# Another seven-product scheme: four products through one PSUM bank that is read in between

## The chip, the core and the metric

The kernel runs on one core of a Trainium2 chip. Its engines work in parallel, each through its own queue in order: TensorE (PE, matmuls into PSUM banks), VectorE (DVE), ScalarE (ACT), GpSimd (POOL, here issuing loads) and SyncE (SP, here issuing stores). The metric is device time in microseconds (us) of one execution; lower is better.

## The reference

```python
scores = scale * np.matmul(q, k.transpose(0, 1, 3, 2))     # q, k, v: (8, 12, 448, 64)
attn = softmax(scores)
x = np.matmul(attn, v).transpose(0, 2, 1, 3).reshape(3584, 768)
h = x @ w_in                                               # (768, 2048)
g = h * (1.0 / (1.0 + np.exp(-h)))
out = g @ w_out                                            # (2048, 768), float32
```

Attention for 8 batches of 12 heads and 448 tokens, then a two-layer network over all 3584 tokens.

## The kernel before, in words

Operands are fp16, sums fp32 in PSUM. Attention for a batch is made in units of four heads: scores (line 336), exponentials on ACT (373), sums and values on PE (399, 415), and a normalisation on DVE (482) into `xT`. For batches 0 to 5 the first layer is plain: six matmuls of 128 x 448 for each of 16 slices f of the hidden layer (496), a tanh on ACT (507), a gate on DVE (543), into the gate buffer `G` (`X` for a few tokens).

**Seven products.** Elsewhere a product of two-by-two blocks is computed with seven block products instead of eight. The blocks are combined by sums beforehand and the seven results are combined afterwards. This is done in two places:

- *the pair stage* (first layer of the last two batches, `PB` = 6 and 7): the blocks are the two batches and the two halves of the 768 inputs against two halves of inputs and hidden slices. For each f from 0 to 7 there are seven products of three matmuls of 128 x 448 (`pair_product`, line 632), copies on ACT (`pair_copy`, 657), sums on DVE (`pair_add`, 663), and four gates on ACT (`silu`, 670). The weight and input sums are `combine_w_in` (608) and `combine_x` (590).
- *the quads* (second layer, 13 of 14 groups of 2 x 128 tokens, `qd` 1 to 13; group 0 is plain, 718): seven products of eight matmuls of 128 x 384 (`product`, 704) with summed weights (`combine_w`, 533) and summed gate outputs (`combine_g`, 694). Three ACT copies (770, 776, 780) and six DVE additions (766) make the four output blocks, which are stored by 32 or 64 tokens (`store`, 762).

A PSUM bank holds one such result. In the pair stage banks A and C are separate one-bank tiles (tag "m", four of them), and B and D are the two halves of a two-bank tile (tag "s", two of them, which hold the scores before). `PBANK` and `BANK` say which product goes into which bank; a product that is not first in its bank adds to what is there.

**What sets the order.** A planner written in Python (`Order`) runs when the program is built. It keeps a clock of its own, assumed durations for every operation, and counts of free buffers and banks (`Ring`). Whenever PE is free it issues the first item of the list `moe` whose dependencies are done and whose buffers are free, or attention work; ACT and DVE take the ready operation with the earliest due time (ready time plus a bias). The engines then get exactly this order. On the chip the semaphores are set by the tile framework from the tiles that the operations read and write, not from the planner's dependencies. Stores are issued by SP, for the last two quads by ACT in turn with SP.

Of the kernel before, what the change touches and what calls it, by code (L numbers as in the profile page):

```python
# [165 lines left out]
def kernel(  # L166
# [42 lines left out]
    NSG, NTMP, NOST = 3, 3, 4  # L209
# [307 lines left out]
    W_ = {m: const.tile([128, HF, OH], FP16, name=f"D{m}") for m in (1, 4, 6)}  # L517
# [4 lines left out]
    }  # L522
    W_[3], W_[7], W_[5], W_[2] = B_[0, 1], B_[1, 0], B_[1, 1], B_[0, 0]

    def combine_w(m, f0, f1):
        i0, i1, op = {
            1: ((0, 0), (1, 1), ALU.add),
            4: ((1, 0), (0, 0), ALU.subtract),
            6: ((0, 0), (0, 1), ALU.add),
            3: ((0, 1), (1, 1), ALU.subtract),  # L530
            7: ((1, 0), (1, 1), ALU.add),
        }[m]
        nc.vector.tensor_tensor(
            out=W_[m][:, f0:f1], in0=B_[i0][:, f0:f1], in1=B_[i1][:, f0:f1], op=op
        )
# [75 lines left out]
    PBANK = {1: "A", 2: "A", 6: "B", 5: "C", 3: "C", 7: "D", 4: "D"}  # L611

    def pair_product(f, m):
        if m in (1, 5):
            pp_t[(f, PBANK[m])] = ps.tile(
                [128, 512], FP32, name=f"f_{f}_{m}", tag="m", bufs=4
            )[:, 0:S]
        elif m == 6:
            two = ps.tile([128, 2, 512], FP32, name=f"f_{f}_{m}", tag="s", bufs=2)
            pp_t[(f, "B")], pp_t[(f, "D")] = two[:, 0, 0:S], two[:, 1, 0:S]  # L620
# [10 lines left out]
        for c in range(3):  # L631
            nc.tensor.matmul(  # L632
                out=pp_t[(f, PBANK[m])],
                lhsT=w[:, c, :],
                rhs=a[:, c, :],
                start=(c == 0 and m in (1, 6, 5, 7)),
                stop=(c == 2),
                skip_group_check=True,
            )

    def pair_tmp(f, name):
# [4 lines left out]
            "v": ("T", NT_, [128, HG, S], FP16),  # L646
        }[name]
        t = sb.tile(shape, dt, name=f"{name}_{f}", tag=tag, bufs=n)
        if len(shape) == 5:
            t = t.rearrange("p c x i e -> p (c x i e)")  # L650
        elif len(shape) == 3:
            t = t.rearrange("p h s -> p (h s)")
# [6 lines left out]
    def pair_add(f, to, x, y):  # L659
        x = pp_t[(f, x)] if x in "BCD" else pf_t[(f, x)]  # L660
        y = pf_t[(f, y)]
        out = pf_t[(f, to)] if (f, to) in pf_t else pair_tmp(f, to)
        nc.vector.tensor_tensor(out=out, in0=x, in1=y, op=ALU.add)
# [13 lines left out]
    S_t, tmp_t, ost_t, pr_t = {}, {}, {}, {}  # L677

    def combine_g(qd, m, f0, f1):
        a, b = 2 * qd, 2 * qd + 1  # L680
        x, y, op = {
            5: (rows(a, 0), rows(a, 1), ALU.add),
            2: (rows(b, 0), rows(b, 1), ALU.add),
            1: (rows(a, 0), rows(b, 1), ALU.add),
            6: (rows(b, 0), rows(a, 0), ALU.subtract),
            7: (rows(a, 1), rows(b, 1), ALU.subtract),
        }[m]
        if m > 5:
            dst = x
        else:  # L690
            if (qd, m) not in S_t:
                S_t[(qd, m)] = sb.tile([128, HF, 128], FP16, name=f"S_{qd}_{m}", tag="S", bufs=NSG)
            dst = S_t[(qd, m)]
        nc.vector.tensor_tensor(out=dst[:, f0:f1], in0=x[:, f0:f1], in1=y[:, f0:f1], op=op)  # L694

    BANK = {3: 3, 5: 3, 4: 4, 2: 4, 1: 1, 7: 1, 6: 6}

    def product(qd, m):
        w = {3: rows(2 * qd, 0), 4: rows(2 * qd + 1, 1), 6: rows(2 * qd + 1, 0), 7: rows(2 * qd, 1)}
# [34 lines left out]
    def tmp(qd, name):  # L734
        tmp_t[(qd, name)] = sb.tile([128, OH], FP32, name=f"{name}_{qd}", tag="tmp", bufs=NTMP)
        return tmp_t[(qd, name)]

# [27 lines left out]
    def add(out, a, b, op=ALU.add):  # L765
        nc.vector.tensor_tensor(out=out, in0=a, in1=b, op=op)  # L766


    def take_3(qd):
        nc.scalar.copy(out=tmp(qd, "s"), in_=bank(qd, 3))  # L770

    def take_4(qd):
        add(tmp_t[(qd, "s")], bank(qd, 4), tmp_t[(qd, "s")])

    def take_5(qd):
        nc.scalar.copy(out=ost(qd, 0, 1), in_=bank(qd, 3))  # L776
        store(qd, 0, 1)

    def take_2(qd):
        nc.scalar.copy(out=ost(qd, 1, 0), in_=bank(qd, 4))  # L780
        store(qd, 1, 0)

    def take_1(qd):
        add(tmp(qd, "m"), bank(qd, 1), tmp_t[(qd, "s")])

    def less_12(qd):
        add(tmp_t[(qd, "s")], tmp_t[(qd, "s")], ost_t[(qd, 0, 1)], ALU.subtract)

    def less_21(qd):
        add(tmp_t[(qd, "m")], tmp_t[(qd, "m")], ost_t[(qd, 1, 0)], ALU.subtract)  # L790

    def take_6(qd):
        add(ost(qd, 1, 1), bank(qd, 6), tmp_t[(qd, "m")])
        store(qd, 1, 1)

    def take_7(qd):
        add(ost(qd, 0, 0), bank(qd, 1), tmp_t[(qd, "s")])
        store(qd, 0, 0)
# [113 lines left out]
    sg_ring, tmp_ring, ost_ring = Ring(NSG), Ring(NTMP), Ring(NOST)  # L912
    far_ring = Ring(NX3)
    STORE = 3.0
    pr_op, sg_op, w_op, plain_op = {}, {}, {2: [], 5: []}, {}
# [3 lines left out]
    def queue_ffn1(b, g0, g1):  # L919
        t0, t1 = 32 * g0, 32 * g1  # L920
        for f in range(NFF) if b == 0 else [x for f in range(HF) for x in (f, f + HF)]:
# [22 lines left out]
            def deps(f=f):  # L944
# [3 lines left out]
                for qd in range(NT * B // 4) if u else ():  # L948
                    if any(t // NT == u - 1 and (r or t % NT < 4) for t in (2 * qd, 2 * qd + 1)):
# [3 lines left out]
                            else [pr_op.get((qd, m)) for m in (3, 4, 6, 7)]  # L953
# [56 lines left out]
    def queue_pair_f(f, xs):  # L1010
        done, lo = {}, f // 4 * 4

        def free(r):
            made = []
            for qd in range(NT * B // 4):
                for t in (2 * qd, 2 * qd + 1):
                    if t // NT == PB // 2 - 1 and t % NT < (4, NT - 1)[r]:
                        made += [pr_op.get((qd, m)) for m in (3, 4, 6, 7)]
# [10 lines left out]
        def queue(m):  # L1029
            rings = {  # L1030
                1: ((rq_ring, 1),),
                6: ((s_ring, 1), (kt_ring, 1), (t_ring, 1)),
                5: ((rk_ring, 1),),
            }.get(m, ())
            ms = (6, 7) if m == 6 else (m,)

            def run():
                op = Op(
                    "PE",
                    3 * len(ms) * mm(S),  # L1040
                    lambda: [pair_product(f, x) for x in ms],
                    tail=PE_OUT,
                )
                if m in (1, 5):
                    m_ring.take()
# [6 lines left out]
                elif m == 6:  # L1052
                    read("u", "DVE", lambda: pair_add(f, "u", "B", "p"), [op, done["p"]])
                    read("v", "DVE", lambda: pair_add(f, "v", "D", "u"), [op, done["u"]])
                elif m == 5:
                    read("q", "ACT", lambda: pair_copy(f, "q", "C"), [op], None, -3)
                    read("22", "DVE", lambda: pair_add(f, "v", "q", "v"), [done["v"], done["q"]], rk_ring.give)
                    gate_of(1, 1, "v", [done["22"]], t_ring.give)
                elif m == 2:
                    gate_of(0, 0, "A", [op], m_ring.give)  # L1060
                elif m == 3:
                    read("12", "DVE", lambda: pair_add(f, "p", "C", "u"), [op, done["u"]], m_ring.give)
                    gate_of(1, 0, "p", [done["12"]], rq_ring.give)
                else:
                    read("21", "DVE", lambda: pair_add(f, "u", "D", "u"), [op, done["12"]], s_ring.give)
                    gate_of(0, 1, "u", [done["21"]], kt_ring.give)

            def deps():
                made = [xs[0, c] for c in (range(3, NDC) if m == 2 else range(3))]
                if m in (5, 6):  # L1070
                    made += [pair_x[i] for i in ((2, 3) if m == 6 else (1,))]
                    made += [pair_w.get((i, lo)) for i in ((2, 3) if m == 6 else (1,))]
                elif m == 3:
                    made.append(pair_x[4])
                elif m == 4:
                    made.append(pair_w.get((4, lo)))
                made += [done.get(x) for x in {2: ["p"], 3: ["q"], 4: ["v"]}.get(m, [])]
                first = {3: (2, 5), 4: (3,), 5: (6,), 6: (1,)}.get(m, ())
                made += [(done.get(x), 9.0) for x in first]
                return made + (free(0) if m == 1 else free(1) if m == 6 else [])  # L1080

            moe.append((deps, int(m in (1, 5)), run, rings))

        for m in (1, 6, 5, 2, 3, 4):
            queue(m)

    def sums_w(ms):

        for m in ms:
# [6 lines left out]
                        ld_wout + list(plain_op.values()) * (m in (3, 7)),  # L1096
# [6 lines left out]
    def queue_plain(t, j):  # L1103
# [6 lines left out]
        def queue(f0, f1):  # L1110
            def run():
# [10 lines left out]
                if len(plain_op) == 4:  # L1122
                    sums_w((3, 7))
# [22 lines left out]
    def plan_sums():  # L1146
# [12 lines left out]
        for m in (5, 2, 1, 6, 7):  # L1159
            sg_op[(qd, m)] = []  # L1160
            for f0 in (0, 4):
                deps = [x for f in range(f0, f0 + 4) for x in gates[f] + gates[f + HF]]
                if m > 5:
                    deps += sg_op[(qd, {6: 2, 7: 5}[m])]
# [12 lines left out]
    def queue_quad(qd):  # L1177
# [4 lines left out]
        def read(m, eng, fn, deps, then=None):  # L1182
            if m in (5, 2):
                then = lambda at: (m_ring.give(at), home.give(at + STORE))
            elif m in (6, 7):
                then = lambda at: (m_ring.give(at), home.give(at + STORE), tmp_ring.give(at))
            busy = act(OH) if eng == "ACT" else OH / 960.0 + 0.13
            bias = -2 if eng == "ACT" else -4
            took[m] = od.add(Op(eng, busy, lambda: fn(qd), deps, bias, then=then))

        def queue(m, first):
            def run():
# [5 lines left out]
                if m in (5, 2, 1):  # L1198
# [3 lines left out]
                if m == 3:  # L1202
                    read(3, "ACT", take_3, [op])
                elif m == 4:
                    read(4, "DVE", take_4, [op, took[3]])
                elif m == 5:
                    read(5, "ACT", take_5, [op], m_ring.give)
                elif m == 2:
# [375 lines left out]
```

## Time and profile before

| | us |
|---|---|
| three runs | 395.9, 396.16, 396.45; median 396.16 |
| profiled execution, span from first to last instruction | 394.4 (its time beyond the span is not given) |
| PE busy | 386.5 (98%) |
| DVE, ACT busy | 311.3 (79%), 243.2 (62%) |
| quad products, L704 / pair products, L632, share of the chain that ended last | 29% / 8% |
| copy of 384 columns on ACT (L776, L780, L770) | 0.48 each |
| copy of 448 columns on ACT (L657) | 0.53 each |
| addition of 384 columns on DVE (L766) | 0.55 each |
| addition of 448 columns on DVE (L663) | 0.62 each |

A row of the profile names the line of the kernel, the engine, the operation, the tile written and the tiles read, then the count and the time. Idle time in front of a row stands in brackets with what ended it. The chain that ended last is the sequence of work that is followed back from the last instruction. A busy PE is not necessarily PE at its peak, since matmuls overlap: a matmul's own duration is longer than the distance to the next one.

### The profile page before, as it was taken

The numbers are of one execution on the slowest core, as the hardware profiler recorded it, in microseconds if no ns is written. First come the engines' busy times: TensorE is split into PE (matmuls) and PEld (weight loads), VectorE is DVE, ScalarE is ACT, GpSimd is POOL, SyncE is SP. The second block draws the span as 40 slices with busy tenths as digits, with TensorE's granted clock in tenths as the row PEclk, the third lists the DMA queues.
The fourth block names the chain that finished last, engine by engine and source line by source line (L and its number), as shares of the span: only waits on it lengthen the run. The fifth ranks groups of instructions, "written<-read, shape, count | busy, mean of one in ns | idle before, by whom it ended". The sixth has DMA issues, their size and how long they took to land.

```text
span 394.4 us, 9273 instructions
## 1 busy us (share of the span) xinstructions
PE 386.5 (98%) x3679; PEld 199.0 (50%) x3679; DVE 311.3 (79%) x653; ACT 243.2 (62%) x378; POOL 83.6 (21%) x153
## 2 busy tenths in 40 slices
PE   7999999999999999999999999999999999999995
PEld 6667764443444444554444444344444555556663
DVE  2466676999999697896888786988879898787863
ACT  4988885696863868626868429686593227872110
POOL 6632546315004242500051221120000000000000
PEclk9999999999999999999999999999999999999999
DMA  7999999919034863582145751531100131001334
GB/s 113 205 210 210 166 179 164 175 36 141 1 76 88 142 95 47 75 158 71 25 49 81 139 109 46 71 48 42 42 1 2 40 87 35 2 1 42 80 82 121
DMA packets 35356, 34.44 MB, mean 87 GB/s; under 512 B 11376, under 2 KB 33776, under 8 KB 35312
## 3 DMA queue, kind: packets, MB, share of 16 engines
q0 software_dynamic: 24784, 22.82, 39.2%
q1 hardware_dynamic: 9952, 10.33, 9.6%
q10 hardware_dynamic: 576, 0.69, 0.6%
q8 instruction: 29, 0.48, 0.5%
q14 instruction: 15, 0.12, 0.1%
HBM read 45.61 MB, written 11.01 MB: 144 GB/s over the span
## 4 chain that ended last, share of the span: by engine, by line
PE 94%; DMA 3%; DVE 1%; ACT 1%; POOL 0%; issue 0%; POOLq 0%
PE p L704 29%; PE h L496 29%; PE s L336 12%; PE a L399 10%; PE f L632 8%; PE o L718 3%; DMA rq<-in_q_dram 3%; PE a L415 2%; PE z L1491 1%; ACT E L373 0%; DVE S L694 0%; POOL rk L249 0%; DVE rq L323 0%; DVE rdn L466 0%; DVE ost L766 0%
## 5 line engine op out<-in xcount | busy, mean ns | idle before, releaser
L373 ACT ACTIVATE E<-s 128x896 f16<-128x896 f32 (+1 forms) x172 | 150.0, 915 | 48.6 <-PE s L336 47.5
L496 PE MATMUL h<-xT,w_in_t 128*128 128x448 f16 (+1 forms) x672 | 118.6, 327 | 0.0
L496 PEld LDWEIGHTS <-w_in_t 128*128 128x128 f16 x672 | 61.2, 98 | 54.0 <-issue 18.0
L507 ACT ACTIVATE th<-h 128x448 f16<-128x448 f32 (+1 forms) x112 | 54.3, 495 | 31.4 <-PE h L496 22.5
L543 DVE SCALAR_TENSOR_TENSOR G<-th,h 128x448 f16<-128x448 f16 (+2 forms) x112 | 55.1, 507 | 15.3 <-ACT th L507 13.3
L270 POOL DMA_DIRECT2D V<-in_v_dram x88 | 48.5, 568 | 56.5 <-PE a L399 42.7
L336 PE MATMUL s<-rq,KT 32*128 32x448 f16 (+4 forms) x768 | 50.9, 337 | 1.4 <-DVE rq L323 0.9
L704 PEld LDWEIGHTS <-G 128*128 128x128 f16 x384 | 36.5, 98 | 28.1 <-issue 4.4
L704 PEld LDWEIGHTS <-S 128*128 128x128 f16 x312 | 29.3, 98 | 23.9 <-issue 5.2
L399 PE MATMUL a<-E,V 128*32 128x448 f16 (+3 forms) x864 | 40.4, 335 | 0.0
L255 POOL DMA_DIRECT2D rq<-in_q_dram x27 | 15.1, 560 | 113.0 <-PE s L336 82.9
L704 PE MATMUL p<-D,G 128*128 128x384 f16 x208 | 37.6, 326 | 0.0
L704 PE MATMUL p<-w_out_t,S 128*128 128x384 f16 x208 | 37.2, 326 | 0.1
L482 DVE SCALAR_TENSOR_TENSOR xT<-a,rdn 128x448 f16<-128x448 f32 (+1 forms) x54 | 28.7, 565 | 7.4 <-PE a L399 6.5
L336 PEld LDWEIGHTS <-KT 32*128 32x128 f16 (+2 forms) x864 | 17.5, 98 | 29.6 <-issue 25.9
L704 PE MATMUL p<-w_out_t,G 128*128 128x384 f16 x176 | 31.9, 326 | 0.0
L399 PEld LDWEIGHTS <-V 128*32 128x32 f16 (+2 forms) x864 | 18.2, 95 | 22.4 <-issue 14.7
L384 DVE TENSOR_TENSOR T<-T,E 128x1792 f16<-128x1792 f16 x20 | 21.8, 1089 | 8.0 <-ACT E L373 7.9
L694 DVE TENSOR_TENSOR S<-G 128x512 f16<-128x512 f16 x70 | 25.3, 414 | 3.2 <-PE p L704 3.0
L384 DVE TENSOR_TENSOR T<-E,E 128x1792 f16<-128x1792 f16 x20 | 21.6, 1082 | 5.6 <-ACT E L373 5.6
L776 ACT COPY ost<-p 128x384 f32<-128x384 f32 x13 | 6.2, 480 | 27.4 <-PE p L704 22.6
L305 DVE STREAM_TRANSPOSE KT<-rk 128x256 f32<-128x256 f32 (+3 forms) x48 | 16.6, 384 | 7.0 <-DMA rk<-in_k_dram 6.2
(74 smaller groups left out, 370.2 us busy)
## 6 DMA issues: line engine op xcount, KB each, us to landing
out_dram<-ost SPq DMA_DIRECT2D x194, 48.0 KB, 1.7
rk<-in_k_dram POOLq DMA_DIRECT2D x24, 224.0 KB, 5.9
rq<-in_q_dram POOLq DMA_DIRECT2D x21, 224.0 KB, 5.2
w_in_t<-in_moe_w_in_dram POOLq DMA_DIRECT2D x6, 512.0 KB, 11.2
w_out_t<-in_moe_w_out_dram POOLq DMA_DIRECT2D x4, 768.0 KB, 13.5
V<-in_v_dram POOLq DMA_DIRECT2D x43, 64.0 KB, 3.9
V<-in_v_dram POOLq DMA_DIRECT2D x40, 48.0 KB, 4.0
out_dram<-ost SPq DMA_DIRECT2D x8, 96.0 KB, 2.2
```

The source lines that it names most:

```text
L270: nc.gpsimd.dma_start(out=VT[b][32 * x : 32 * (x + 1), hs, 0:count, :], in_=v[b, hs].rearrange("h (i g) d -> i h g d", g=TPP)[:, :, first ...
L336: nc.tensor.matmul(out=pS[p0 : p0 + 32 * (x1 - x0), h % 2, at : at + nq], lhsT=KT[(b, hg)][32 * h : 32 * (h + 1), c, x0:x1, :, e], rhs=QT[ ...
L373: nc.scalar.activation(out=E[(n, w)][0:kr, 2 * y : 2 * y + 2, 0:nk], in_=pS_t[(n, w, y)][0:kr, :, 0:nk], func=AF.Exp, scale=attn_scale,)
L384: nc.vector.tensor_tensor(out=T[n], in0=T[n] if step else E[(n, 0)], in1=E[(n, step + 1)], op=ALU.add,)
L399: nc.tensor.matmul(out=a[32 * h : 32 * (h + 1), 0:nq], lhsT=w, rhs=e[k0:k1, h, at : at + nq], start=start, stop=stop,)
L482: nc.vector.scalar_tensor_tensor(out=x3(b, cc)[:, cc % 3, 32 * g0 : 32 * g1], in0=acc[(n, part)][:, 0:nq], scalar=0.5, in1=rdn_t[n].rearra ...
L496: nc.tensor.matmul(out=h[:, 0 : t1 - t0], lhsT=w_in_t[:, cc, 128 * f : 128 * (f + 1)], rhs=x3(b, cc)[:, cc % 3, t0:t1], start=(cc == 0), s ...
L507: nc.scalar.activation(out=th, in_=h_t[(b, f, t0)][:, 0 : t1 - t0], func=AF.Tanh)
L543: nc.vector.scalar_tensor_tensor(out=dst[:, f, at + lo : at + hi], in0=th_t[(b, f, t0)][:, lo - t0 : hi - t0], scalar=1.0, in1=h_t[(b, f, ...
L632: nc.tensor.matmul(out=pp_t[(f, PBANK[m])], lhsT=w[:, c, :], rhs=a[:, c, :], start=(c == 0 and m in (1, 6, 5, 7)), stop=(c == 2), skip_gro ...
L694: nc.vector.tensor_tensor(out=dst[:, f0:f1], in0=x[:, f0:f1], in1=y[:, f0:f1], op=op)
L704: nc.tensor.matmul(out=pr_t[(qd, BANK[m])][:, 0:OH], lhsT=w[:, f, :], rhs=W_[m][:, f, :], start=(f == 0 and BANK[m] == m), stop=(f == HF - 1),
```

## The change

The seven products are formed after another scheme, in both places. Its sums build on one another: a second sum is made from the first one and a third from the second. In the quads four sums of gate outputs take the place of five and four sums of weights the place of five. Products 1, 6, 7 and 4 follow one another in one bank. Its content is read after 1, after 6 (1 + 6), after 7 (1 + 6 + 7) and after 4 (all four). Product 2 has a bank of its own, and 5 and 3 share one. Three DVE additions per quad (for 2, 7, 3) and four ACT copies (for 1, 5, 6, 4) take the place of six and three.

In the pair stage the same scheme is used: three copies (p after 1, u after 6, q after 5) and three additions (p += B after 2, q += A after 7, u += C after 3) take the place of two and five. Banks A (1, 6, 7, 4) and B (2) are the halves of the two-bank tile, and C (5, 3) is a one-bank tile; bank D is gone.

The planner's queueing follows: one item per product, in the order 1, 5, 6, 2, 7, 3, 4. The output buffers `ost` grow from four to seven and the three `tmp` buffers go.

```diff
-    NSG, NTMP, NOST = 3, 3, 4
+    NSG, NOST = 3, 7
...
-    W_[3], W_[7], W_[5], W_[2] = B_[0, 1], B_[1, 0], B_[1, 1], B_[0, 0]
+    W_[1], W_[2], W_[3], W_[7] = B_[0, 0], B_[1, 0], B_[1, 1], B_[0, 1]
...
+            5: (B_[0, 1], B_[0, 0]),
+            6: (B_[1, 1], W_[5]),
+            4: (B_[1, 0], W_[6]),
+            7: (B_[1, 1], B_[0, 1]),
...
-    PBANK = {1: "A", 2: "A", 6: "B", 5: "C", 3: "C", 7: "D", 4: "D"}
+    PBANK = {1: "A", 6: "A", 7: "A", 4: "A", 2: "B", 5: "C", 3: "C"}
...
-        if m in (1, 5):
-            pp_t[(f, PBANK[m])] = ps.tile(
-                [128, 512], FP32, name=f"f_{f}_{m}", tag="m", bufs=4
-            )[:, 0:S]
-        elif m == 6:
+        if m == 5:
+            pp_t[(f, "C")] = ps.tile([128, 512], FP32, name=f"f_{f}_{m}", tag="m", bufs=4)[:, 0:S]
+        elif m == 1:
             two = ps.tile([128, 2, 512], FP32, name=f"f_{f}_{m}", tag="s", bufs=2)
-            pp_t[(f, "B")], pp_t[(f, "D")] = two[:, 0, 0:S], two[:, 1, 0:S]
+            pp_t[(f, "A")], pp_t[(f, "B")] = two[:, 0, 0:S], two[:, 1, 0:S]
...
-    def pair_add(f, to, x, y):
-        x = pp_t[(f, x)] if x in "BCD" else pf_t[(f, x)]
-        y = pf_t[(f, y)]
-        out = pf_t[(f, to)] if (f, to) in pf_t else pair_tmp(f, to)
-        nc.vector.tensor_tensor(out=out, in0=x, in1=y, op=ALU.add)
+    def pair_add(f, to, x):
+        t = pf_t[(f, to)]
+        nc.vector.tensor_tensor(out=t, in0=pp_t[(f, x)], in1=t, op=ALU.add)
...
+            5: (rows(b, 0), rows(b, 1), ALU.add),
+            6: (S_t.get((qd, 5)), rows(a, 0), ALU.subtract),
+            7: (rows(a, 0), rows(b, 0), ALU.subtract),
+            3: (rows(a, 1), S_t.get((qd, 6)), ALU.subtract),
...
-    BANK = {3: 3, 5: 3, 4: 4, 2: 4, 1: 1, 7: 1, 6: 6}
+    BANK = {1: 1, 6: 1, 7: 1, 4: 1, 2: 2, 5: 5, 3: 5}
...
+    OUT = {1: (0, 0), 5: (1, 1), 6: (0, 1), 4: (1, 0)}
+    SUM = {2: (0, 0), 7: (1, 1), 3: (0, 1)}
+
+    def take_copy(qd, m):
+        nc.scalar.copy(out=ost(qd, *OUT[m]), in_=bank(qd, BANK[m]))
+        if m == 4:
+            store(qd, *OUT[m])
+
+    def take_sum(qd, m):
+        t = ost_t[(qd, *SUM[m])]
+        nc.vector.tensor_tensor(out=t, in0=bank(qd, BANK[m]), in1=t, op=ALU.add)
+        store(qd, *SUM[m])
...
             rings = {
-                1: ((rq_ring, 1),),
-                6: ((s_ring, 1), (kt_ring, 1), (t_ring, 1)),
+                1: ((s_ring, 1), (rq_ring, 1)),
                 5: ((rk_ring, 1),),
+                6: ((kt_ring, 1),),
             }.get(m, ())
...
+                elif m == 6:
+                    read("u", "ACT", lambda: pair_copy(f, "u", "A"), [op], None, -3)
                 elif m == 2:
-                    gate_of(0, 0, "A", [op], m_ring.give)
+                    read("11", "DVE", lambda: pair_add(f, "p", "B"), [op, done["p"]])
+                    gate_of(0, 0, "p", [done["11"]], rq_ring.give)
+                elif m == 7:
+                    read("22", "DVE", lambda: pair_add(f, "q", "A"), [op, done["q"]])
+                    gate_of(1, 1, "q", [done["22"]], rk_ring.give)
                 elif m == 3:
-                    read("12", "DVE", lambda: pair_add(f, "p", "C", "u"), [op, done["u"]], m_ring.give)
-                    gate_of(1, 0, "p", [done["12"]], rq_ring.give)
+                    read("12", "DVE", lambda: pair_add(f, "u", "C"), [op, done["u"]], m_ring.give)
+                    gate_of(1, 0, "u", [done["12"]], kt_ring.give)
                 else:
-                    read("21", "DVE", lambda: pair_add(f, "u", "D", "u"), [op, done["12"]], s_ring.give)
-                    gate_of(0, 1, "u", [done["21"]], kt_ring.give)
+                    gate_of(0, 1, "A", [op, done["11"]], s_ring.give)
...
+                made += [
+                    done.get(x)
+                    for x in {6: ["p"], 7: ["u", "q"], 3: ["q"], 4: ["22", "11"]}.get(m, [])
+                ]
...
-        for m in (1, 6, 5, 2, 3, 4):
+        for m in (1, 5, 6, 2, 7, 3, 4):
             queue(m)
```

More of the change, by code (lines that the diff above doesn't have):

```diff
@@ L516 @@
     X = const.tile([128, NFF, 128], FP16, name="X")
-    W_ = {m: const.tile([128, HF, OH], FP16, name=f"D{m}") for m in (1, 4, 6)}
+    W_ = {m: const.tile([128, HF, OH], FP16, name=f"D{m}") for m in (4, 5, 6)}
     B_ = {
@@ L522 @@
     }
-    W_[3], W_[7], W_[5], W_[2] = B_[0, 1], B_[1, 0], B_[1, 1], B_[0, 0]
+    W_[1], W_[2], W_[3], W_[7] = B_[0, 0], B_[1, 0], B_[1, 1], B_[0, 1]
     def combine_w(m, f0, f1):
[L526 to L531, printed above, removed]
+        x, y = {
+            5: (B_[0, 1], B_[0, 0]),
+            6: (B_[1, 1], W_[5]),
+            4: (B_[1, 0], W_[6]),
+            7: (B_[1, 1], B_[0, 1]),
         }[m]
         nc.vector.tensor_tensor(
-            out=W_[m][:, f0:f1], in0=B_[i0][:, f0:f1], in1=B_[i1][:, f0:f1], op=op
+            out=W_[m][:, f0:f1], in0=x[:, f0:f1], in1=y[:, f0:f1], op=ALU.subtract
         )
@@ L635, in pair_product @@
                 rhs=a[:, c, :],
-                start=(c == 0 and m in (1, 6, 5, 7)),
+                start=(c == 0 and m in (1, 2, 5)),
                 stop=(c == 2),
@@ L645, in pair_tmp @@
             "u": ("KT", 3, [128, NCH, 4, 32, 2], FP16),
-            "v": ("T", NT_, [128, HG, S], FP16),
         }[name]
@@ L650, in pair_tmp @@
             t = t.rearrange("p c x i e -> p (c x i e)")
-        elif len(shape) == 3:
-            t = t.rearrange("p h s -> p (h s)")
         pf_t[(f, name)] = t[:, 0 : 2 * S].bitcast(FP32)
@@ L675, in silu @@
         )
-    S_t, tmp_t, ost_t, pr_t = {}, {}, {}, {}
+    S_t, ost_t, pr_t = {}, {}, {}
     def combine_g(qd, m, f0, f1):
         a, b = 2 * qd, 2 * qd + 1
+        if m != 7 and (qd, m) not in S_t:
+            S_t[(qd, m)] = sb.tile([128, HF, 128], FP16, name=f"S_{qd}_{m}", tag="S", bufs=NSG)
         x, y, op = {
[L682 to L686, printed above, removed]
-        }[m]
[L688 to L693, printed above, removed]
+            5: (rows(b, 0), rows(b, 1), ALU.add),
+            6: (S_t.get((qd, 5)), rows(a, 0), ALU.subtract),
+            7: (rows(a, 0), rows(b, 0), ALU.subtract),
+            3: (rows(a, 1), S_t.get((qd, 6)), ALU.subtract),
+        }[m]
+        dst = rows(b, 0) if m == 7 else S_t[(qd, m)]
         nc.vector.tensor_tensor(out=dst[:, f0:f1], in0=x[:, f0:f1], in1=y[:, f0:f1], op=op)
-    BANK = {3: 3, 5: 3, 4: 4, 2: 4, 1: 1, 7: 1, 6: 6}
+    BANK = {1: 1, 6: 1, 7: 1, 4: 1, 2: 2, 5: 5, 3: 5}
     def product(qd, m):
-        w = {3: rows(2 * qd, 0), 4: rows(2 * qd + 1, 1), 6: rows(2 * qd + 1, 0), 7: rows(2 * qd, 1)}
+        w = {1: rows(2 * qd, 0), 2: rows(2 * qd, 1), 4: rows(2 * qd + 1, 1), 7: rows(2 * qd + 1, 0)}
         w = w[m] if m in w else S_t[(qd, m)]
@@ L732, in bank @@
         return pr_t[(qd, m)][:, 0:OH]
-    def tmp(qd, name):
-        tmp_t[(qd, name)] = sb.tile([128, OH], FP32, name=f"{name}_{qd}", tag="tmp", bufs=NTMP)
-        return tmp_t[(qd, name)]
     def ost(qd, i, j):
@@ L763, in store @@
             w, turn = w + n, turn + 1
[L765 to L798, printed above, removed]
+    OUT = {1: (0, 0), 5: (1, 1), 6: (0, 1), 4: (1, 0)}
[8 more added lines that the diff above has]
+        store(qd, *SUM[m])
     units = []
@@ L911 @@
     ffn1_left = {b: 0 for b in range(B)}
-    sg_ring, tmp_ring, ost_ring = Ring(NSG), Ring(NTMP), Ring(NOST)
+    sg_ring, ost_ring = Ring(NSG), Ring(NOST)
     far_ring = Ring(NX3)
     STORE = 3.0
-    pr_op, sg_op, w_op, plain_op = {}, {}, {2: [], 5: []}, {}
+    pr_op, sg_op, w_op, plain_op = {}, {}, {1: [], 2: [], 3: []}, {}
     inv_op, norm_op = [], []
@@ L952, in deps @@
                             if qd == 0
-                            else [pr_op.get((qd, m)) for m in (3, 4, 6, 7)]
+                            else [pr_op.get((qd, m)) for m in (1, 2, 3, 4, 7)]
                         )
@@ L1017, in free @@
                     if t // NT == PB // 2 - 1 and t % NT < (4, NT - 1)[r]:
-                        made += [pr_op.get((qd, m)) for m in (3, 4, 6, 7)]
+                        made += [pr_op.get((qd, m)) for m in (1, 2, 3, 4, 7)]
             return made
@@ L1030, in queue @@
             rings = {
-                1: ((rq_ring, 1),),
-                6: ((s_ring, 1), (kt_ring, 1), (t_ring, 1)),
+                1: ((s_ring, 1), (rq_ring, 1)),
                 5: ((rk_ring, 1),),
+                6: ((kt_ring, 1),),
             }.get(m, ())
-            ms = (6, 7) if m == 6 else (m,)
             def run():
[L1038 to L1044, printed above, removed]
+                op = Op("PE", 3 * mm(S), lambda: pair_product(f, m), tail=PE_OUT)
+                if m == 5:
                     m_ring.take()
@@ L1051, in run @@
                     read("p", "ACT", lambda: pair_copy(f, "p", "A"), [op], None, -3)
-                elif m == 6:
-                    read("u", "DVE", lambda: pair_add(f, "u", "B", "p"), [op, done["p"]])
-                    read("v", "DVE", lambda: pair_add(f, "v", "D", "u"), [op, done["u"]])
                 elif m == 5:
                     read("q", "ACT", lambda: pair_copy(f, "q", "C"), [op], None, -3)
-                    read("22", "DVE", lambda: pair_add(f, "v", "q", "v"), [done["v"], done["q"]], rk_ring.give)
-                    gate_of(1, 1, "v", [done["22"]], t_ring.give)
+                elif m == 6:
+                    read("u", "ACT", lambda: pair_copy(f, "u", "A"), [op], None, -3)
@@ L1068, in deps @@
             def deps():
                 made = [xs[0, c] for c in (range(3, NDC) if m == 2 else range(3))]
[L1070 to L1082, printed above, removed]
-        for m in (1, 6, 5, 2, 3, 4):
+                i = {5: 1, 6: 2, 7: 3, 3: 4}.get(m)
+                if i:
+                    made.append(pair_x[i])
+                i = {5: 1, 6: 2, 7: 3, 4: 4}.get(m)
+                if i:
+                    made.append(pair_w.get((i, lo)))
@@ L1085, in queue_pair_f @@
+                made += [
+                    done.get(x)
+                    for x in {6: ["p"], 7: ["u", "q"], 3: ["q"], 4: ["22", "11"]}.get(m, [])
+                ]
+                return made + (free(0) if m == 1 else free(1) if m == 5 else [])
+            moe.append((deps, int(m == 5), run, rings))
+        for m in (1, 5, 6, 2, 7, 3, 4):
             queue(m)
@@ L1095, in sums_w @@
                         lambda m=m, f0=f0: combine_w(m, f0, f0 + 4),
-                        ld_wout + list(plain_op.values()) * (m in (3, 7)),
+                        ld_wout
+                        + list(plain_op.values()) * (m == 7)
+                        + [w_op[k][f0 // 4] for k in {6: (5,), 4: (6,)}.get(m, ())],
                         30,
@@ L1122, in run @@
                 if len(plain_op) == 4:
-                    sums_w((3, 7))
+                    sums_w((7,))
             def deps():
@@ L1158, in plan_sums @@
         sg_ring.take(3)
-        for m in (5, 2, 1, 6, 7):
+        for m in (5, 6, 7, 3):
             sg_op[(qd, m)] = []
@@ L1162, in plan_sums @@
                 deps = [x for f in range(f0, f0 + 4) for x in gates[f] + gates[f + HF]]
-                if m > 5:
-                    deps += sg_op[(qd, {6: 2, 7: 5}[m])]
+                if m != 5:
+                    deps += sg_op[(qd, {6: 5, 7: 5, 3: 6}[m])]
                 sg_op[(qd, m)].append(
@@ L1180, in queue_quad, with read, then, queue @@
         home = far_ring if qd in FAR else ost_ring
[L1182 to L1186, printed above, removed]
+        def read(m, deps):
+            def then(at):
+                if m in (2, 3, 4):
+                    m_ring.give(at)
+                if m in (2, 3, 4, 7):
+                    home.give(at + STORE)
+            fn, eng = (take_copy, "ACT") if m in OUT else (take_sum, "DVE")
             busy = act(OH) if eng == "ACT" else OH / 960.0 + 0.13
             bias = -2 if eng == "ACT" else -4
-            took[m] = od.add(Op(eng, busy, lambda: fn(qd), deps, bias, then=then))
-        def queue(m, first):
+            took[m] = od.add(Op(eng, busy, lambda: fn(qd, m), deps, bias, then=then))
+        def queue(m):
+            first = {6: (1,), 2: (1,), 7: (6, 5), 3: (5, 6, 7), 4: (7,)}.get(m, ())
             def run():
@@ L1197, in run @@
                     ring.take(need)
-                if m in (5, 2, 1):
+                if m in (5, 6, 3):
                     op.then = sg_ring.give
@@ L1201, in run @@
                 pr_op[(qd, m)] = op
[L1202 to L1208, printed above, removed]
-                    read(2, "ACT", take_2, [op], m_ring.give)
-                elif m == 1:
-                    read(1, "DVE", take_1, [op, took[4]])
-                    read("less_12", "DVE", less_12, [took[1], took[5]])
-                    read("less_21", "DVE", less_21, [took[1], took[2]])
-                elif m == 6:
-                    read(6, "DVE", take_6, [op, took["less_21"]], m_ring.give)
-                else:
-                    read(7, "DVE", take_7, [op, took["less_12"]], m_ring.give)
@@ L1219, in deps @@
-            def deps():
-                made = list(w_op.get(m, [None])) + [x for y in first if y for x in [took.get(y)]]
-                if m in (3, 4):
-                    t = 2 * qd + m - 3
+                read(m, [op] + [took[x] for x in {2: (1,), 7: (5,), 3: (6,)}.get(m, ())])
+            def deps():
+                made = list(w_op.get(m, [None]))
+                hard = {6: (1,), 7: (6,), 3: (5,), 4: (7,)}.get(m, ())
+                made += [took.get(x) if x in hard else (took.get(x), 9.0) for x in first]
+                if m in (1, 2, 4):
+                    t = 2 * qd + m // 4
+                    i = int(m != 1)
@@ L1223, in deps @@
                     for b in {(128 * t + c) // S for c in (0, 127)}:
                         for f in range(HF):
-                            x = g_op.get((b, f + HF * (m - 3)), [None])
+                            x = g_op.get((b, f + HF * i), [None])
                             made += [(y, f * mm(OH)) for y in x]
                     return made + ld_wout
-                if m in (1, 6, 7):
-                    made += [pr_op.get((qd, x)) for x in ((5, 2) if m == 1 else (1,))]
                 x = sg_op.get((qd, m), [None, None])
@@ L1231, in deps @@
                 return made + [x[0], (x[1], 4 * mm(OH))]
-            rings = {3: ((tmp_ring, 1),), 1: ((tmp_ring, 1),), 4: ()}
-            rings = rings.get(m, ((home, 1),))
+            rings = ((home, 1),) if m in OUT else ()
             moe.append((deps, 1 if BANK[m] == m else 0, run, rings))
-        for m, first in ((3, ()), (4, (3,)), (5, (3,)), (2, (4,)), (1, ()), (6, ()), (7, (1,))):
-            queue(m, first)
+        for m in (1, 5, 6, 2, 7, 3, 4):
+            queue(m)
     def after_x(n):
@@ L1258, in after_x @@
         if b == 0:
-            sums_w((1, 4, 6))
+            sums_w((5, 6, 4))
             for j in range(2):
```

## The prediction

> **What bounds the kernel now.** I read the page's busy and chain parts first, then the stretches of the second half, the waits of the PE queue, and last the order of the instructions in a timeline around PE's one late stall.
>
> ```profile
> PE 386.5 (98%) x3679; PEld 199.0 (50%) x3679; DVE 311.3 (79%) x653; ACT 243.2 (62%) x378; POOL 83.6 (21%) x153
> ...
> PE 94%; DMA 3%; DVE 1%; ACT 1%; POOL 0%; issue 0%; POOLq 0%
> ```
>
> PE is busy for all but 7.9 us of the span of 394.4 us. DVE and ACT work beside it, so what the change takes from DVE is worth nothing in itself. Where are PE's 7.9 us? By stretch (columns: PE, PEld, DVE, ACT, POOL busy; granted clock; DMA share; GB/s):
>
> ```profile
> 0.00:20.00 20.00, 17.64 (x290) 13.07 (x292) 7.18 (x28) 13.92 (x16) 12.97 (x25) 1.00 1.03 159
> ...
> 300.00:320.00 20.00, 19.43 (x163) 10.57 (x161) 18.07 (x40) 4.93 (x10) 0.00 (x0) 1.00 0.13 34
> 320.00:340.00 20.00, 20.00 (x110) 10.57 (x108) 16.82 (x29) 12.28 (x25) 0.00 (x0) 1.00 0.18 46
> 340.00:360.00 20.00, 20.00 (x114) 10.89 (x112) 15.70 (x31) 13.57 (x26) 0.00 (x0) 1.00 0.01 1
> 360.00:380.00 20.00, 20.00 (x125) 12.05 (x124) 14.08 (x36) 3.35 (x7) 0.00 (x0) 1.00 0.37 95
> 380.00:394.40 14.40, 9.87 (x61) 5.74 (x59) 7.86 (x18) 0.96 (x2) 0.00 (x0) 0.96 0.33 91
> ```
>
> 2.4 us lie in the start and 4.5 us behind the last product (389.87 us) in the last stretch; neither has seven-product work to save. From 60 to 389 us only some 0.7 us are idle, of which 0.57 us have one place: a product that waits for a bank until ACT has copied it out.
>
> ```profile
> 307.77 1.47 PE L704 MATMUL p<-w_out_t,S 128*128 128x384 f16 x8
> ...
> 309.28 0.48 ACT L780 COPY ost<-p 128x384 f32<-128x384 f32 x1 [2.27 <-PE p L704]
> ...
> 309.81 1.46 PE L704 MATMUL p<-D,S 128*128 128x384 f16 x8 [0.57 <-ACT ost L780]
> ```
>
> These three lines give every latency I need: the product ends at 309.24, its reader starts 0.04 us later, takes 0.48, and PE goes on 0.05 us after it. Unhindered, the next product follows after 1.30 us (at 309.07); the stall is 0.74 us, of which the profile prints 0.57 as idle because matmuls overlap.
>
> ```profile
> 322.83 29.51 PE f L632 x156
> 352.34 1.30 PE p L704 x8
> ```
>
> From the chain: 156 matmuls of the pair stage in 29.51 us are 0.189 us each, 0.568 us for a product of three (whose last matmul ends 0.73 us after the product's start); eight of 384 columns are 1.30 us. The pair stage runs today without one gap.
>
> **The change part by part, and the sum.**
>
> *PE's own work.* 3679 matmuls before and after, of the same shapes. In the order of the built program PE moves once more from full products to attention columns and back (14 such changes for 13); the trace has 0.253 us instead of 0.163 us from a product's last matmul to an attention matmul: +0.1 us.
>
> *DVE.* Removed: 39 adds of 384 (0.55), 26 gate sums (0.414), 16 adds of 448 (0.62) and two weight sums (0.93), 44 us in all. *ACT.* Added: 13 copies of 384 (0.48) and 8 of 448 (0.53), 10.5 us. Both lie beside a busy PE. What PE can gain from a lighter DVE is its small late waits: the 1.32 us of gate sums in the chain at 221.75 us cost 0.27 us of PE (start-to-start distances there), and a late X gate at 295.9 us 0.15 us. Ends: both go (-0.4) or both stay, or others like them come (+0.4). I take 0, since ACT gets heavier as DVE gets lighter.
>
> *The old stall at 309 us.* In the new order the bank it waited for is taken early enough (two full products lie between the copy and the next user): -0.74 us.
>
> *Reading a bank between products* is not new in itself: product 2 follows 1 and product 3 follows 5 in one bank today, and the 29.51 us contain that. It costs when less PE work lies between than end + 0.04 + read + 0.05. In the quads at least one product of 1.30 us lies between everywhere but once: in the last quad (13) product 7 stands directly behind 6, as nothing else is left. That is the 309 us stall again, copy of 384 between two products: +0.74 us.
>
> *The pair stage* (PE order and waits read from the built program; durations COPY 0.53 and TENSOR_TENSOR 0.62 of the L657 and L663 rows). Banks A and B are now halves of one tile, and the waits are kept per tile, not per bank. The planner issues the copy u (bank A after product 6) when it thinks 6 is done; product 2, into bank B of the same tile, already stands on PE by then, so the copy waits for product 2's last matmul. The sum p += B waits for that copy, and product 7, back into A, waits for the sum. For f = 4 to 7 PE's order is 6, 2, 3, 7. From the start of 2: it ends at 0.73, copy 0.77 to 1.30, sum 1.34 to 1.96, product 7 at 2.01 instead of 1.14 (2 and 3 being 0.568 each): 0.87 us. Four times: 3.5 us. For f = 2 and 3 the order differs: 2 waits for the copy after 1, with only 5 between (0.73 + 0.04 + 0.53 + 0.05 = 1.35 against 1.14: 0.21); 6, sum, copy, 7 (0.73 + 0.04 + 0.62 + 0.04 + 0.53 + 0.05 = 2.01 against 1.70: 0.31); 2 of f = 3 behind the copy after 6 (0.21); 4 of f = 3 behind two sums on DVE (1.97 against 1.70: 0.26). Together 1.0 us. f = 0 and 1 have over 1.1 us between everywhere: 0. Pair stage: +4.5 us. Behind the waiting matmul stands all of PE; nothing can pass it. ACT has slack then: 3 copies and 4 gates per f are 3 x 0.53 + 4 x 0.57 = 3.9 us in a period that grows from 3.98 to 4.85. If the waits of one f overlapped the next, the cost could not exceed these, because 1 of the next f follows 7 and needs nothing later than 7.
>
> *The end.* The last store follows an ACT copy (0.48) instead of a DVE add (0.56): -0.1 us. DMAs are the same in number and size; ACT and SP share the last ones as before. The ring of seven output buffers leaves every copy's buffer stored over 1.5 us early, with four issues of 0.48 us and 1.7 us to landing per store.
>
> Sum: 0.1 + 0 - 0.7 + 0.7 + 4.5 - 0.1 = +4.5 us. The span would be 398.9 us. The profiled execution is known by its span alone; the median of the three runs, 396.16, is 1.76 us above it, and I keep that distance: 400.6 us.
>
> **A page's rule against the trace.** At the start 47 zero matmuls of 128 columns take 4.24 us, 0.09 us each, where the pair stage's pace would give 0.054; behind the 0.57 us idle of 309 us the next product still takes 1.46 us, so one such gap changes no pace. The Trainium skill, "TensorE: Matmul & The Clock Gate", section "A second HAM failure mode: psum-queue depth-cycling", says that PE idling often between matmul groups as PSUM banks cycle makes the clock oscillate between half and full, which speaks against this change. The trace agrees as far as half pace at a cold start goes; for repeated short gaps no run here shows it. It is rival 3.
>
> **The rivals.**
>
> 1. *The other side: the copy after 6 does not wait for 2 in effect.* If it started when 6 ends, it would be done 1.35 us after 6's start, and 7 stands 1.70 us behind 6: the 0.87 us vanish, f = 2 and 3 lose at most their two 0.21. Then +0.1 - 0.7 + 0.7 - 0.1 + 0.0 to 0.4, with up to -0.4 from DVE: 396.2 us, no change. It decides from the point at which the copy's wait counts 6 and not 2. For it: the planner's own dependencies say exactly this. Against: the built program's wait names the last matmul of 2. Chance 0.07.
> 2. *ACT holds up the reads in the attention stages.* Copies of nine quads stand in one queue with exponentials of 0.915 us (L373), 18 of them between products of one bank. With one product between, the slack is 1.30 + 1.30 - 1.47 - 0.57 = 0.56; an exponential just begun delays by up to 0.36 beyond it. If the rows' busy share of ACT (62%) met a quarter of them with half that, it is 0.8 us; all of them, 6.5 us. Against: in most of them attention blocks lie between as well. With 3 us: 403.5 us. Chance 0.08.
> 3. *PE's pace falls in the pair stage.* At half pace for half of its 168 matmuls: 84 x 0.189 = 16 us, 416 us. Against: the line at 309.81. Chance 0.03.
>
> **How the numbers follow.** My forecast has 0.82: 400.6 us, by its own terms (DVE's ±0.4, ±0.5 on eight stalls of which each is made of four rows) 399.6 to 401.7. To leave out no more than 2 in 10 the range reaches up into rival 2 and a little down: 399.3 to 402.6. Within 0.2% (0.8 us, about what a measurement of this kernel can tell from no change) lies rival 1's centre, and a part of it below with both DVE waits gone: same 0.05, faster 0.02, slower 0.93.
>
> **What the changed profile would show.** PE idle in front of the pair product's matmul line, with a DVE add as releaser, four times about 0.7 us printed, between some 325 and 355 us; f matmuls spread over some 34 us instead of 29.5. One idle of 0.57 us before a p matmul near the end, released by an ACT copy, and none at 309 us. DVE busy near 267 us, ACT near 254 us, PE busy unchanged within 1 us. If PE shows no idle in the pair stage, rival 1 is right and the per-tile wait is where I erred; if the p and h stretches between 100 and 320 us show PE waiting for ACT copies, it is rival 2; if f matmuls stand more than 0.2 us apart without a releaser, rival 3.

## The result and the profile after

The changed kernel takes 400.53 us (median; 400.3 to 400.94), the kernel before beside it 396.29 us: a ratio of 1.011, 95% interval 1.0096 to 1.0124. The forecast was 400.6 us. The profiled execution has a span of 398.6 us, against 394.4.

The busy and chain parts of the changed kernel's page:

```profile
PE 387.6 (97%) x3679; PEld 198.7 (50%) x3679; DVE 273.0 (68%) x570; ACT 252.9 (63%) x399; POOL 83.6 (21%) x153
...
PE 94%; ACT 2%; DVE 1%; DMA 1%; issue 1%; DVEq 0%; ACTq 0%; POOLq 0%
```

DVE has 38 us less to do and ACT 10 us more, and neither number is the result. PE's busy time moves by 1 us. What is new in the chain that ended last are pieces of the pair stage: its sums on DVE (L655, 0.8% of the span) and its copies on ACT (L651, 0.7%). The waits of PE's own queue say where (engine and line, who ended the wait: us in total, times, longest; the three lines left out are waits of the first 60 us):

```profile
PE f L629 <- DVE p L655: 3.0, 4, 0.8
...
PE p L692 <- ACT ost L753: 0.6, 1, 0.6
...
PE f L629 <- ACT u L651: 0.2, 1, 0.2
PE f L629 <- DVE q L655: 0.2, 1, 0.2
```

The first line is new: four waits of a pair product (now line 629) for the sum p += B. So are the last two, shorter waits of the same stage. The waits for `rq`, `zeros` and `E` at the start are there in both kernels. By stretch (busy time of PE, PEld, DVE, ACT, POOL; granted clock; DMA share; GB/s):

```profile
320.00:340.00 20.00, 19.45 (x103) 9.74 (x101) 11.58 (x19) 14.63 (x29) 0.00 (x0) 1.00 0.11 30
340.00:360.00 20.00, 17.04 (x91) 8.72 (x90) 9.80 (x20) 14.66 (x29) 0.00 (x0) 1.00 0.01 1
```

The kernel before had PE busy for 20.00 of 20 us in both rows. From 300 to 320 us, where it had 19.43, the changed kernel has 20.00: the stall of 309 us is gone. One slice f of the pair stage shows the mechanism; the timeline from 338 us:

```profile
338.11 1.30 PE L629 MATMUL f<-sx,tw 128*128 128x448 f16 x6
...
339.24 0.73 PE L629 MATMUL f<-xT,w_in_t 128*128 128x448 f16 x3
...
339.81 0.73 PE L629 MATMUL f<-sx,w_in_t 128*128 128x448 f16 x3
340.06 0.53 ACT L651 COPY u<-f 128x448 f32<-128x448 f32 x1 [0.60 <-PE f L629]
...
340.63 0.62 DVE L655 TENSOR_TENSOR p<-f,p 128x448 f32<-128x448 f32 x1 [2.61 <-ACT u L651]
...
341.31 0.73 PE L629 MATMUL f<-sx,tw 128*128 128x448 f16 x3 [0.77 <-DVE p L655]
```

The first row is products 5 and 6, the second product 2 (into bank B), the third product 3, the last product 7. The copy u reads bank A, which product 6 had completed at 339.41; it starts at 340.06, 0.09 us after product 2 has ended at 339.97. The sum waits for the copy, PE waits for the sum, and 7 starts 0.93 us after its place at 340.38. The idle time printed, 0.77, is smaller by the 0.16 us by which matmuls overlap.

The other idle time of PE stands near the end, in the last quad:

```profile
386.93 2.76 PE L692 MATMUL p<-D,S 128*128 128x384 f16 x16
...
389.73 0.48 ACT L753 COPY ost<-p 128x384 f32<-128x384 f32 x1 [0.82 <-PE p L692]
390.26 1.46 PE L692 MATMUL p<-w_out_t,G 128*128 128x384 f16 x8 [0.57 <-ACT ost L753]
```

It is the stall of 309 us in another place: product 7 stands directly behind 6, whose copy has to be through first.

### The profile page after: what moved, and what is told of

Same layout as the page of the kernel before. It is cut to its first block, busy times and chain, and to the rows that moved or that the text cites. A ratio compares the mean times of both kernels' runs of the same rounds, so it can differ in the third digit from the quotient of the medians.

```text
span 398.6 us, 9252 instructions
## 1 busy us (share of the span) xinstructions
PE 387.6 (97%) x3679; PEld 198.7 (50%) x3679; DVE 273.0 (68%) x570; ACT 252.9 (63%) x399; POOL 83.6 (21%) x153
## 4 chain that ended last, share of the span: by engine, by line
PE 94%; ACT 2%; DVE 1%; DMA 1%; issue 1%; DVEq 0%; ACTq 0%; POOLq 0%
PE p L692 30%; PE h L496 29%; PE s L336 13%; PE a L399 10%; PE f L629 7%; PE o L706 3%; PE a L415 2%; DMA rk<-in_k_dram 1%; DVE p L655 1%; PE z L1439 1%; ACT u L651 1%; ACT E L373 1%; ACT G L662 0%; ACT ost L753 0%; ACT p L651 0%
## 5 line engine op out<-in xcount | busy, mean ns | idle before, releaser
L753 ACT COPY ost<-p 128x384 f32<-128x384 f32 x52 | 25.0, 480 | 66.0 <-PE p L692 56.6
L692 PE MATMUL p<-w_out_t,G 128*128 128x384 f16 x280 | 49.2, 326 | 0.6 <-ACT ost L753 0.6
L759 DVE TENSOR_TENSOR ost<-p,ost 128x384 f32<-128x384 f32 x39 | 21.6, 553 | 33.0 <-PE p L692 19.7
L692 PE MATMUL p<-D,S 128*128 128x384 f16 x208 | 37.0, 326 | 0.0
L629 PE MATMUL f<-sx,tw 128*128 128x448 f16 x72 | 16.4, 352 | 3.2 <-DVE p L655 3.0
```

Of the source, the lines that this page charges most:

```text
L629: nc.tensor.matmul(out=pp_t[(f, PBANK[m])], lhsT=w[:, c, :], rhs=a[:, c, :], start=(c == 0 and m in (1, 2, 5)), stop=(c == 2), skip_group_ ...
L692: nc.tensor.matmul(out=pr_t[(qd, BANK[m])][:, 0:OH], lhsT=w[:, f, :], rhs=W_[m][:, f, :], start=(f == 0 and BANK[m] == m), stop=(f == HF - 1),
L753: nc.scalar.copy(out=ost(qd, *OUT[m]), in_=bank(qd, BANK[m]))
```

## The experiments

The question was which property of the change costs 4.2 us. My theory: the waits follow the tiles, and A and B are one tile. The first rival: it costs to read a bank between products. The second: the quads, with their fourth ACT copy, are to blame.

**A tile of its own for bank B.** The reads of bank A between its products stay as they are.

```diff
-        if m == 5:
-            pp_t[(f, "C")] = ps.tile([128, 512], ..., tag="m", bufs=4)[:, 0:S]
+        if m in (2, 5):
+            t = ps.tile([128, 512], FP32, name=f"f_{f}_{m}", tag="m", bufs=4)
+            pp_t[(f, PBANK[m])] = t[:, 0:S]
         elif m == 1:
             two = ps.tile([128, 2, 512], FP32, name=f"f_{f}_{m}", tag="s", bufs=2)
-            pp_t[(f, "A")], pp_t[(f, "B")] = two[:, 0, 0:S], two[:, 1, 0:S]
+            pp_t[(f, "A")] = two[:, 0, 0:S]
...
-            moe.append((deps, int(m == 5), run, rings))
+            moe.append((deps, int(m in (2, 5)), run, rings))
```

The planner gives this bank back when p += B is done, and issues 2 only behind 1 and 3 only behind 6.

> The pair stage as in the changed kernel, but bank B (product 2) is a one-bank tile of its own, so that it shares no tile with bank A. Bank A is still read after products 1, 6 and 7. My theory (the waits are kept per tile): the waits of product 7 for the sum p += B go, PE has no idle time in the pair stage, 4.8 us less than the changed kernel's 400.5: about 395.8 us; the one idle of 0.57 us near the end stays. Rival (reading a bank between its products is what costs): the reads are the same, so the idle time stays and the time is about 400.5 us.

Measured: 395.97 us, ratio to the kernel before 0.9994 (0.9984 to 1.0003). All of PE's waits that the profile lists:

```profile
PE z L1444 <- DVE zeros L222: 1.0, 1, 1.0
PE p L693 <- ACT ost L754: 0.6, 1, 0.6
PE s L336 <- ACT E L373: 0.4, 1, 0.4
```

The chain of this kernel has the pair stage in one piece:

```profile
322.30 29.60 PE f L630 x156
```

156 matmuls in 29.60 us, where the kernel before needs 29.51. The same products, reads and sums without the shared tile lose 0.1 us, so reading a bank between its products is not what costs.

The planner's order changes with the tile, and one could credit the order. The last two slices settle it, since they stand in the order 6, 2, 3, 7 of the changed kernel; one of them:

```profile
344.93 1.30 PE L630 MATMUL f<-sx,tw 128*128 128x448 f16 x6
...
346.06 0.73 PE L630 MATMUL f<-xT,w_in_t 128*128 128x448 f16 x3
346.26 0.53 ACT L652 COPY u<-f 128x448 f32<-128x448 f32 x1
346.63 0.73 PE L630 MATMUL f<-sx,w_in_t 128*128 128x448 f16 x3
...
346.90 0.62 DVE L656 TENSOR_TENSOR p<-f,p 128x448 f32<-128x448 f32 x1 [2.21 <-PE f L630]
...
347.20 0.73 PE L630 MATMUL f<-sx,tw 128*128 128x448 f16 x3
```

The copy starts 0.03 us after product 6 has ended (346.23), while product 2 runs on until 346.79, and product 7 starts 0.57 us behind 3, before the sum p += B has ended. In the same order the changed kernel lost 0.9 us.

**The copy written ahead of product 2.** In the changed kernel the planner writes the copy u later than product 2, and one could hold that this order of writing is the fault and not the tile.

```diff
+                def emit():
+                    pair_product(f, m)
+                    if m == 6:
+                        pair_copy(f, "u", "A")
+
-                op = Op("PE", 3 * mm(S), lambda: pair_product(f, m), tail=PE_OUT)
+                op = Op("PE", 3 * mm(S), emit, tail=PE_OUT)
...
-                    read("u", "ACT", lambda: pair_copy(f, "u", "A"), [op], None, -3)
+                    read("u", "ACT", lambda: None, [op], None, -3)
```

> The tiles of the changed kernel, but the copy u of bank A is written into the program directly behind product 6, ahead of product 2; PE's order is the same. Theory (per tile): the wait only changes sides. Product 2, though it writes bank B, now waits for the copy of bank A: from the start of 6 0.73 + 0.04 + 0.53 + 0.05 = 1.35 us against 0.57, a stall of 0.78 us, and product 7 still waits for the sum, 1.44 against 1.14, 0.30 us; together 1.08 us for f = 4 to 7 where it was 0.87: about 401.3 us, with PE waiting for ACT copies in front of product 2. Rival (the tracker knows banks, and the late copy came from its place in the order alone): stalls of the pair stage gone but for f = 2 and 3, about 396.5 us.

Measured: 401.42 us, ratio 1.0127 (1.011 to 1.0144). PE in one slice of f (6, 2 and 7, each of three matmuls; 3, between 2 and 7, is left out):

```profile
344.18 0.73 PE L629 MATMUL f<-sx,tw 128*128 128x448 f16 x3
345.53 0.73 PE L629 MATMUL f<-xT,w_in_t 128*128 128x448 f16 x3 [0.62 <-ACT u L651]
...
347.04 0.73 PE L629 MATMUL f<-sx,tw 128*128 128x448 f16 x3 [0.22 <-DVE p L655]
```

Product 2, which writes bank B, now waits for a copy that reads bank A. Whichever of the two is written first, the other waits. The wait costs nothing only where enough work of PE lies between, as for f = 0 and 1 of the changed kernel.

**One half of the change alone.** Two kernels: the quads and weight sums of the change with the pair stage of before, and the reverse. The first takes `PBANK`, `pair_product` to `pair_add` and `queue_pair_f`'s `queue` from the kernel before; the second takes them from the change, with product 2 issued only behind 1.

> The quads and weight sums of the changed kernel with the pair stage of the kernel before. Theory: the quads' part is worth next to nothing although it takes 32 us of additions and gate sums from DVE, since PE is the bound; the wait between products 6 and 7 of the last quad (0.74 us) stays, and in the new order one of quad 9 with nothing between 6 and 7 comes, 0.74 us and 0.4 us behind it, where the kernel before had 0.74 us at 309 us: about 1 us above the kernel before, 397.2 us. Rival (ACT's four copies per quad hold up PE in the attention stages): above 399 us, with PE waiting for ACT copies between 100 and 300 us.

> The pair stage of the changed kernel with the quads and weight sums of the kernel before. Theory: five slices with the order 6, 2, 3, 7 at 0.87 us each, and 0.5 us at the others: about 4.8 us above the kernel before, 401.1 us. Rival (the quads cause the loss): about 396.3 us.

Measured: the quads alone 397.06 us, ratio 1.002 (1.0011 to 1.0029); the pair stage alone 401.09 us, ratio 1.0121 (1.0106 to 1.0136). The quads alone, PE's waits for copies and for `xT`:

```profile
PE p L699 <- ACT ost L760: 1.1, 2, 0.6
...
PE f L631 <- DVE xT L482: 0.5, 1, 0.5
```

The two copies are those of quad 9 and quad 13, where nothing stands between 6 and 7; the wait for `xT` follows quad 9's at 319 us. Between 100 and 300 us, where seven quads with four copies each run among the exponentials (the last of which starts at 294.6), PE is never idle (same columns as above):

```profile
100.00:300.00 200.00, 200.00 (x1825) 90.33 (x1824) 152.76 (x297) 136.47 (x202) 38.77 (x71) 1.00 0.41 69
```

The pair stage alone:

```profile
PE f L630 <- DVE p L656: 3.9, 6, 0.8
```

Five products 7 lose 0.9 us each instead of four, because the planner falls into the order 6, 2, 3, 7 one slice earlier; the sixth wait is a shorter one, a loss of 0.4 us. So the pair stage alone brings all that the change loses. The quads' copies cost PE only where 7 stands directly behind 6, and none of them among the exponentials. The halves (+0.8 and +4.9) add up to more than the whole (+4.2): the stall at quad 9 and the fifth long wait are in the halves alone, where PE's order is another.

**Bank B beside C.** Another test of the same rule: the half that B shares is changed, not removed. A becomes a one-bank tile, allocated with product 1; C and B are the halves of the other, allocated with product 5. The planner issues 2 only behind 5.

```diff
-            pp_t[(f, "A")], pp_t[(f, "B")] = two[:, 0, 0:S], two[:, 1, 0:S]
+            pp_t[(f, "C")], pp_t[(f, "B")] = two[:, 0, 0:S], two[:, 1, 0:S]
```

> Bank B moves from the tile of bank A into the tile of bank C; A is a one-bank tile. Theory (per tile): the wait of 7 for p += B goes, but a smaller one comes: the sum p += B now waits for product 3, which writes the other half of its tile, the sum q += A stands behind it on DVE, and product 4 behind that: 0.2 us for each f. With 0.74 and 0.4 us at quad 9, where 7 stands directly behind 6 in this order: about 399 us, between the changed kernel (400.5) and the version with a tile for B alone (396.0). Rival (only the reads of A count): 400.5 us.

Measured: 399.63 us, ratio 1.0088 (1.0075 to 1.0101). The 0.9 us waits of product 7 are gone and product 4 comes late instead, by 0.31 us for each of f = 4 to 7 (start-to-start distances of PE beyond 0.189 us), where I had 0.2. The sign and the place came as expected; the size was 0.6 us short in all. PE's order is not that of the changed kernel here either: PE waits for the copies of quads 9 and 13 (0.57 us each) and for `xT` (0.5 us), as with the quads alone.

**The last stall, too.** With bank B's own tile, product 2 of the last quad is kept until 6 has been issued, so that it separates 6 and 7.

```diff
+                if m == 2 and 4 * qd + 4 == NT * B:
+                    made.append((pr_op.get((qd, 6)), 9.0))
```

> Bank B in its own tile, and in the last quad product 2 is held back until 6 has been issued, so that it stands between 6 and 7. Theory: the last stall (0.74 us) goes as well, no idle of PE is left that a copy or sum ends: 0.74 us less than with bank B's own tile alone (395.97), 395.2 us, about 0.25% below the kernel before. Rival (the end is set by the last stores): the time stays at 396.0 us.

Measured: 395.23 us, ratio 0.9982 (0.9974 to 0.9991): 0.2% below the kernel before. The waits that are left to PE in the profile's list are those of the start alone (for `zeros`, `rq` and `E`).

**What DVE's and ACT's load is worth.** Both are tried on this last kernel, with work that writes the same values again; the planner does not know of it, so the order stays the same.

```diff
-        nc.vector.tensor_tensor(out=dst[:, f0:f1], in0=x[:, f0:f1], in1=y[:, f0:f1], op=op)
+        for _ in range(1 if m == 7 else 2):
+            nc.vector.tensor_tensor(out=dst[:, f0:f1], in0=x[:, f0:f1], in1=y[:, f0:f1], op=op)
```

> As the version with B's own tile and the mended end, but six of the eight gate sums of each quad are made twice (the second writes the same values): 78 more DVE operations of 0.41 us, 32 us. It asks what DVE's load is worth. If DVE had the 10% of free time that its busy share suggests everywhere, 395.2 us. Theory: it is free only where no normalisation of attention (L482) or transpose stands behind the sums; at about five places PE would wait for one, 0.4 to 0.9 us each: about 398.7 us.

Measured: 398.99 us, ratio 1.0071 (1.0057 to 1.0086), 3.8 us above its base of 395.23.

```profile
PE f L630 <- DVE xT L482: 1.0, 1, 1.0
...
PE a L399 <- DVE xT L482: 0.9, 1, 0.9
PE h L496 <- DVE xT L482: 0.7, 1, 0.7
...
PE p L694 <- DVE xT L482: 0.4, 1, 0.4
PE p L694 <- DVE sT L452: 0.4, 1, 0.4
```

With DVE at 76% of the span, 69% in its base, PE already waits, each time for attention's normalisation or transpose. The quad copies, made twice:

```diff
+        nc.scalar.copy(out=o, in_=bank(qd, BANK[m]))
         nc.scalar.copy(out=o, in_=bank(qd, BANK[m]))
```

> As the version with B's own tile and the mended end, but each of the four ACT copies of a quad is made twice, so that PE's next product into that bank waits 0.43 us longer, and ACT has 25 us more to do. It asks how far the reads between products are from costing. Theory: one product of 1.30 us between leaves 0.56 us of slack, so only three places lose 0.1 to 0.2 us: 395.7 us. Rival (ACT's queue holds up the reads in the attention stages): above 397 us.

Measured: 395.93 us, ratio 0.9997 (0.9988 to 1.0006), 0.7 us above its base. The three small losses are in PE's start distances: products at 164.65, 175.97 and 317.59 us each start 0.05 us after a second copy has ended, 0.12, 0.11 and 0.11 us later than in the base. They are too short for the profile's list of waits. At 319.06 us a gap shrinks by 0.10 us, so 0.2 us stay. The larger part is at the end: from PE's last matmul to the end of the span it takes 4.78 us instead of 4.28, since the last store stands behind the second copy of product 4 (0.48 us).

## Why the prediction was right, step by step

The spans differ by 4.2 us; the terms below, most of them start-to-start distances of PE beyond the undisturbed pace, add up to 4.3. The range and the mechanism held; that 400.53 us came within 0.1 us of 400.6 is luck, since errors of 0.1 to 0.3 us in single terms cancel.

- *The pair stage, +4.5.* Measured +4.8. Product 7 of f = 4 to 7 lost 0.93, 0.88, 0.93 and 0.88 us (forecast 0.87 each); the four waits of f = 2 and 3 were 0.22, 0.38, 0.27 and 0.35 (forecast 0.21, 0.31, 0.21, 0.26). The forecast was 0.3 us too small, mostly by one hop: at five of the eight waits the first reader started 0.09 to 0.10 us after the product's end and not 0.04 us. Why the hop differs is not settled. The mechanism is shown by the two runs on the tile and the order of writing.
- *The stall at 309 us, -0.7, and the one at the end, +0.7.* Both as forecast, 0.73 each.
- *DVE's small waits, 0.* The one at 222.7 us (0.27) went, the one at 295 us stayed, and one of 0.14 us came at 321 us: -0.1. So 38 us less on DVE gained PE a tenth of a microsecond. The converse is not true: 30 us more cost 3.8 us in an order that did not allow for them. The forecast had 44 us less on DVE, added up from mean durations of single operations; these overlap where they follow closely (two gate sums of 0.41 us each are 0.75 us of busy time, as in the changed kernel at 386.31). It changes nothing in the forecast time.
- *The additional change to attention columns, +0.1.* As forecast (one more, 0.093 us).
- *The end, -0.1.* Measured -0.2, from PE's last matmul to the end of the span: 4.5 us before, 4.3 after.
- *Not in the forecast, -0.3:* PE reached its 1250th matmul 0.3 us earlier (95.26 against 95.54). The order of PE is the same up to there; the other runs, with the same start, lie between 95.00 and 95.64, so this is how far the start varies.
- *Rival 1* (the copy does not wait for 2 in effect) fell with the copy's row at 340.06. Its time was right for the kernel that it described: own tile, forecast 396.2, measured 395.97.
- *Rival 2* (ACT holds up the reads in the attention stages) fell: in the changed kernel too PE is busy for 200.00 of 200 us from 100 to 300 us. Its price was also too high, since seven quads and not nine have their copies among exponentials.
- *Rival 3* (PE's pace falls): behind idle times of 0.7 to 0.8 us every 4.85 us, three matmuls still take 0.73 us and the next product follows 0.56 us later, at a granted clock of 1.00. The oscillation that the Trainium skill ("TensorE: Matmul & The Clock Gate", section "A second HAM failure mode: psum-queue depth-cycling") describes for PE idling between matmul groups did not come with gaps of this size. The 0.09 us of the zero matmuls at the start is a mean of two paces: in the kernel before, some 30 distances of 0.107 us come first, then 0.056.

## What to carry to other kernels

When one engine is busy for 98% of the span, a change that relieves the others is to be judged by the waits that it puts in front of that engine, and these can be counted before a run: for each wait, the work that lies between against the end, hop, read and hop. Look for two independent banks in one tile: in these kernels their reads and writes wait for one another, in whichever order they are written, and the planner's own dependencies do not show it. A quad product whose bank must be read first needs one other product of 1.30 us before it, also at the end of the list, where nothing is left unless something is kept back.

## What was not expected

Copying four of the results of each quad twice gives ACT 23 us more, and PE lost only 0.2 us by it: one product of 1.30 us in between covers all but about 0.1 us of a doubled read. The half microsecond at the end, where the last store waits for the second copy, was not in the forecast. DVE is much less forgiving than its share of 69% suggests: the run with the doubled gate sums was forecast at 398.7 us from the places where attention waits, and took 398.99.
